# Attention scores before the spectral products: one wide pair and three single banks, two scan banks, and the division and the maxima's last steps at other places

## The chip, the cores and the metric

The kernel runs on one core of one Trainium2 chip. The metric is the device time of one execution in microseconds, given as the median of several executions. The traces are profiled executions of the same program.

## The reference

Two branches of a model are mixed by a gate, for 2048 rows of width 512 in float32:

```python
def reference(A_x, A_wqkv, A_wo, B_x, B_dft_seq_re, B_dft_seq_im, B_dft_hid_re, B_dft_hid_im, gate_w):
    x = A_x
    g = _sigmoid((x * gate_w).sum(-1, keepdims=True))
    # A: 32 heads of width 16
    q, k, v = ...                                  # x @ wqkv, cut into heads
    p = _softmax(einsum("bhqd,bhkd->bhqk", q, k) * 16 ** -0.5)
    a = einsum("bhqk,bhkd->bhqd", p, v) ... @ wo
    # B: Fourier mixing, the real part
    re = einsum("bsd,ed->bse", x, dft_hid_re)
    im = einsum("bsd,ed->bse", x, dft_hid_im)
    b = einsum("ts,bse->bte", dft_seq_re, re) - einsum("ts,bse->bte", dft_seq_im, im)
    return g * a + (1 - g) * b
```

## The kernel before, in words

The program has three parts. In the first, up to about 340 us, the projections to queries, keys and values and the first Fourier product are made, and beside them the first maxima of scores ("scans") for the softmax. Most products work on values split into a high and a low part of a narrower float format, so that one product becomes three matmuls of 64 rows each.

The second part is attention, 16 pairs of heads one after the other. A pair has 32 **steps**: two halves of the queries (1024 each) times 16 blocks of 128 keys. In a step the scores of the two heads (j = 0 and 1) against two chunks of 512 queries (c = 0 and 1) are made by four matmuls (L690), in the order that `ORDERS` gives: "e0" is the next score of head 0, "c0" the next scan of head 0, "s0" the next spectral matmul of row half 0. Head 0 uses rows 0 to 49 of the array, head 1 rows 64 to 113, so that two neighbours run beside each other. The scores go to PSUM, an exponential on ScalarE (`exponentials`, L672) takes them to SBUF, and `pv` (L702, "the value product") multiplies them with the values, summing over the keys in bank `pvb`. The value product of a step is issued after the scores of the second step behind it. Two steps are a **macro**, numbered m from 0 to 255.

A **scan** (L723) makes the scores of 128 queries against 512 keys, and VectorE reduces them to their maximum (L725). Scans run ahead of the pairs that use them. When a pair is scanned, `shift` gives five pieces of work: a reduction (L209), a transposition (L210), a cast (L211), a subtraction (L212) on VectorE, and a store of two DMAs on SyncE (L206). They are put on the list `late`, and the main loop takes them from it between the tokens of a macro. The query rows of a pair are loaded only when its scan is done, with a margin while `late` holds anything.

The first 42 macros (`SINGLES`) are 84 **single steps**: "e0 e1 c0 c1 e0 e1", then a value product, with no spectral matmuls. They use the pool `wide` of PSUM: two pairs of banks ("a" for chunk 0, "b" for chunk 1), each emptied by one exponential of 1024 columns, three single banks in turn for scans, and the bank `pvb`: eight in all. From macro 42 on `narrow()` replaces the pool: scores and scans share five banks that a planner of the program (`Banks`) hands out, each exponential takes 512 columns, and between the scores stand the spectral matmuls (L946) with two banks of their own, z0 and z1, in groups; `closing` holds groups that ended in a macro, and `group.close` has VectorE read their bank out (L855, L857, and L891 for the output product).

At the end of each half of a pair, `quotients` copies `pvb` to SBUF (`ob`, L735 on VectorE in the single steps, L737 on ScalarE later) and GpSimd gathers the sums by DMA (`lc<-ob`, L740). `divide` gives three pieces that the main loop runs at the head of a later macro, by the list `staged`: `invert` (a reciprocal on VectorE, L747, which waits for the gather, and a DMA, L748), `spread` (four DMAs on GpSimd, L752) and `scale` (three GpSimd operations, L755, L762 and L763, and two stores, L770, or for pair 14 the loads of its rows).

From macro 234 on the groups are the product with wo. `output_operands` loads its parts on SyncE; two of these tiles are first cleared (L791), then filled by four DMAs each (L793).

In the third part, after the last step, the last products are made and the rows are stored.

Of the kernel before, what the change touches and what calls it, by code (L numbers as in the profile page):

```python
# [10 lines left out]
F32 = mybir.dt.float32  # L11
# [7 lines left out]
P = 128  # L19
# [4 lines left out]
NP = H // 2  # L24
# [18 lines left out]
SINGLES = 42  # L43
# [17 lines left out]
def build(tc, x, xT, wqkv, wo, wrT, wiT, cr, ci, gate, out):  # L61
    nc = tc.nc
    with ExitStack() as ctx:
# [534 lines left out]
        with ExitStack() as pa:  # L598
# [6 lines left out]
            wide = pw.enter_context(tc.tile_pool(name="wide", bufs=1, space=PSUM, reuse_waits="tile"))  # L605
            pools = []

            def bank(tag, name="s"):
                return pools[0].tile([P, 512], F32, tag=tag, name=name)
# [11 lines left out]
            for s in range(NB - 4, NB):  # L621
                raw = ap.tile([P, D], F32, tag="take", name="abr", bufs=3)
# [36 lines left out]
            banks = Banks()  # L659
            es, waiting = {}, []  # L660
# [13 lines left out]
            pair = {}  # L674
# [3 lines left out]
            def score(j):  # L678

                step, c = divmod(scores[j], 2)  # L680
                scores[j] += 1
                p, h, kb, b = step // PERIODS, step % PERIODS // NB, step % NB, 64 * j
                rows, alone = used[p], step < 2 * SINGLES
                if alone:
                    if c not in pair:
                        pair[c] = wide.tile([P, 1024], F32, tag="ab"[c], name="s2")
                    ps = pair[c][:, j * 512:j * 512 + 512]
                else:
                    ps = bank(banks.take("e", j))
                nc.tensor.matmul(ps, rows.k[kb // 8][b:b + 50, kb % 8 * P:(kb % 8 + 1) * P],  # L690
                                 rows.q[h][b:b + 50, c * 512:c * 512 + 512], start=True, stop=True)
                es.setdefault(step, {})
                if alone and scores[1 - j] <= 2 * step + c:
                    return
                waiting.append((step, c, None, pair.pop(c)) if alone else (step, c, j, ps))
                exponentials()

            def pv(step):
                p, h, kb = step // PERIODS, step % PERIODS // NB, step % NB
                banks.step()  # L700
                for c, j, r in quads:
                    nc.tensor.matmul(pvb[r:r + VC, :], va[:, kb, 2 * p + j, :], es[step][c][0][:, j * 512:j * 512 + 512],  # L702
                                     start=kb == 0, stop=kb == NB - 1, tile_position=(0, r))
                unused.extend(i for e, i in es.pop(step).values())
                exponentials()
                if kb == NB - 1 and step < STEPS - 1:
                    m = step // 2 + 1
                    for n, f in zip((3, 6, 9) if m < SINGLES else (2, 4, 6) if p < NP - 1 else (2, 3, 4), divide(*quotients(p, h))):
                        staged.setdefault(m + n, []).append(f)

            scans, late, leaving = [FRONT, FRONT], [], []
# [1 line left out]
            def scan(j):  # L713

                n = scans[j]
                scans[j] += 1
                p, i = n // SCANS, n % SCANS
                qb, c, b = i // 4, i % 4, 64 * j
                rows = scanned[p]
                if p not in mx:  # L720
                    new_maxima(p)
                ps = wide.tile([P, 512], F32, tag=f"c{(2 * n + j) % 3}", name="s") if now[0] < SINGLES else bank(banks.take("c", j))
                nc.tensor.matmul(ps, rows.q[qb // 8][b:b + 48, qb % 8 * P:(qb % 8 + 1) * P],  # L723
                                 rows.k[c // 2][b:b + 48, c % 2 * 512:(c % 2 + 1) * 512], start=True, stop=True)
                nc.vector.tensor_reduce(mx[p][:, j, qb, c:c + 1], ps, axis=AX.X, op=ALU.max)  # L725
                if i == SCANS - 1 and min(scans) > n:
                    late.extend(shift(p))
                    leaving.extend(("scan", p, part) for part in ("k0", "k1", "q1"))
                elif i == SCANS // 2 - 1 and min(scans) > n:
                    leaving.append(("scan", p, "q0"))  # L730
# [49 lines left out]
            def output_operands():  # L780

                for n in range(2 * ND - 2):
                    b = [block(6 + 2 * n + i) for i in range(2)]
                    raw = (ap.tile([P, D], F32, tag="craw", name="wor", bufs=3) if n == ND - 2 else
                           ap.tile([P, D], F32, tag="take", name="wor", bufs=3))
                    if n < ND - 1:
                        nc.sync.dma_start(raw, wo[n * P:n * P + P, :].rearrange("(h e) m -> e h m", e=DH))
                    else:
                        base = D - (8, 4, 2)[n - ND + 1] * DH
                        if n >= ND:  # L790
                            nc.vector.memset(raw, 0.0)  # L791
                            for c, j, r in quads:
                                nc.sync.dma_start(raw[r:r + DH, :], wo[base + DH * j:base + DH * j + DH, :])  # L793
                        else:
                            for r in (0, 64):
                                nc.sync.dma_start(raw[r:r + 64, :],
                                                  wo[base:base + 64, :].rearrange("(h e) m -> e h m", e=DH))
                    raws_.append((raw, b))
                    if n % (ND - 1) == ND - 2:
                        yield  # L800
                        yield
                        for raw, b in raws_:
                            yield
                            nc.vector.tensor_copy(b[0], raw)
                            nc.vector.tensor_sub(b[1], raw, b[0].bitcast(F32))
                            (w2 if n < ND - 1 else w4).append(b)
                        raws_.clear()
                        yield
# [247 lines left out]
            for m in range(MACROS):  # L1056
                for step in (2 * m, 2 * m + 1):
                    part_b(step)
                now[0] = m
                for f in staged.pop(m, ()):  # L1060
                    f()
                if m == SINGLES - 1:
                    for _ in range(3):
                        load_unit(ap, "craw", 3)
                if m == SINGLES:
                    narrow()
                release(*leaving)
                leaving.clear()
                p, half = divmod(m, NB)
                if half == NB // 2:  # L1070
                    leaving.append(("use", p, "q0"))
                elif half == 0 and m:
                    leaving.extend(("use", p - 1, part) for part in ("k0", "k1", "q1"))
                prefetch(m)
                for ph, s in freed:
                    if ph == 0:
                        renew(s)
                    else:
                        if s == 2:
                            output_rows(0)  # L1080
                        if s == 11:
                            output_rows(1)
                        if s in (5, 7, 9, 10, 11, 12):
                            next(operands, None)
                freed.clear()
                if m >= OUTM:
                    next(operands, None)
                n = min(scans)
                want = planned(m)
                ready = min(TOTAL, scans_ready(m))  # L1090
                count_ = max(0, min(2 if m < SINGLES else 4, want - n, ready - n))
                if m < SINGLES:
                    for i in range(2):
                        for k, token in enumerate(ORDERS[(count_ + 1 - i) // 2].split()):
                            {"e": score, "c": scan}[token[0]](int(token[1]))
                            if late and k == 3:
                                late.pop(0)()
                        values(2 * m + i - 1)
                    continue
                for k, token in enumerate(ORDERS[count_, sizes[m]].split()):  # L1100
                    {"e": score, "c": scan, "s": fill}[token[0]](int(token[1]))
                    if late and k in (6, 13, 20):
                        late.pop(0)()
                for group, j, ps in closing:
                    group.close(j, ps)
                closing.clear()
                values(2 * m)
            assert min(scans) == TOTAL, scans
# [85 lines left out]
```

## Time and profile before

| | |
|---|---|
| median of three runs | 1720.14 us (1719.69 to 1720.67) |
| profiled execution | 1721.4 us, span 1719.6 us |
| mean granted clock of TensorE | 0.996 |
| busy: PE, PEld, DVE, ACT, POOL | 1700.7, 1006.6, 1240.3, 1351.3, 696.2 us |
| exponentials (L672) | 1880: 168 of 1024 columns, 1712 of 512 columns |
| scans in attention (L723, L725) | 1312 |
| first and last start of an exponential | 342.0 and 1700.3 us |

The span is the time from the first to the last instruction of the profiled execution. PE is TensorE's matmuls, PEld its weight loads, DVE VectorE, ACT ScalarE, POOL GpSimd and SP SyncE. A matmul that waits for its weights counts as busy. In a row of the timeline stand start and length in us, engine, line, operation, tiles (what is written, then what is read), the shape, the count of merged instructions, and in brackets the idle time of the engine before it with what ended it. In rows of waits stand the one that waited, whom it waited for, the sum in us, the times and the longest.

### The profile page before, as it was taken

To read this page: it belongs to the slowest core of one execution; us is meant where nothing else is said; L and a number is where in the kernel's file an instruction comes from. 1 tells how busy PE (TensorE), PEld (TensorE's weight loads), DVE (VectorE), ACT (ScalarE), POOL (GpSimd) and SP (SyncE) were. 2 spreads that over 40 slices of the span, in tenths; PEclk is the share of its full clock that TensorE was granted. 3 is DMA by queue.
4 is the path that set the end of the run, shared out by engine and by line. 5 is a ranking of instruction groups with operands and counts; after the bars stand their busy time and mean duration, and the time that the engine had idled before them with its cause. 6 is when DMAs were issued, how large, how long until landed. Compare 5 with 4: busy or idle time off the path is not lost.

```text
span 1719.6 us, 37003 instructions
## 1 busy us (share of the span) xinstructions
PE 1700.7 (99%) x13687; PEld 1006.6 (59%) x13687; DVE 1240.3 (72%) x2359; ACT 1351.3 (79%) x2447; POOL 696.2 (40%) x876
## 2 busy tenths in 40 slices
PE   9999999999999999999999999999999999999998
PEld 7777778733335555565555555555555555555554
DVE  5699899866677777777777777777777777776333
ACT  5689988799997777777777777777777777777785
POOL 1464201444564544444444444434444443443121
PEclk9999999999999999999999999999999999999999
DMA  7664234553352333232333256323332322335422
GB/s 277 224 231 156 70 121 142 176 177 124 116 155 83 95 99 96 64 110 69 88 88 95 75 164 206 107 82 106 97 95 87 119 78 86 113 93 162 128 55 100
DMA packets 140005, 206.61 MB, mean 120 GB/s; under 512 B 58848, under 2 KB 61392, under 8 KB 139824
## 3 DMA queue, kind: packets, MB, share of 16 engines
q1 hardware_dynamic: 97552, 173.76, 31.8%
q0 software_dynamic: 41696, 29.44, 6.4%
q8 instruction: 108, 1.77, 0.4%
q10 hardware_dynamic: 576, 1.05, 0.2%
q14 instruction: 73, 0.60, 0.1%
HBM read 137.89 MB, written 65.81 MB: 118 GB/s over the span
## 4 chain that ended last, share of the span: by engine, by line
PE 93%; DMA 1%; issue 1%; DVE 1%; ACT 1%; POOL 0%; SPq 0%; DVEq 0%; ACTq 0%; POOLq 0%
PE pvb L702 27%; PE z L946 21%; PE s L723 15%; PE s L690 14%; PE xy L342 5%; PE s L187 5%; PE xy L358 5%; DMA q_d<-el 0%; ACT e L672 0%; DVE y L891 0%; DMA wor<-wo 0%; DMA lc<-ob 0%; POOL xg L546 0%; DMA qs<-q_d 0%; PE s L219 0%
## 5 line engine op out<-in xcount | busy, mean ns | idle before, releaser
L672 ACT ACTIVATE e<-s 128x512 f32<-128x512 f32 (+1 forms) x1880 | 1064.4, 638 | 262.2 <-PE s L690 211.5
L725 DVE TENSOR_REDUCE mx<-s 128x1 f32<-128x512 f32 x1312 | 849.6, 687 | 328.8 <-PE s L690 220.5
L690 PE MATMUL s<-qs,ks 50*128 50x512 f32 x2048 | 645.3, 425 | 0.9 <-ACT e L672 0.7
L702 PE MATMUL pvb<-e,va 128*17 128x512 f32 x4096 | 497.9, 596 | 0.0
L723 PE MATMUL s<-ks,qs 48*128 48x512 f32 x1312 | 484.8, 418 | 1.2 <-DVE mx L725 0.7
L946 PE MATMUL z<-b,chi 64*128 64x512 f32 x2060 | 472.0, 392 | 0.0
L690 PEld LDWEIGHTS s<-qs,ks 50*128 50x128 f32 x2048 | 325.6, 185 | 159.3 <-ACT e L672 138.9
L723 PEld LDWEIGHTS s<-ks,qs 48*128 48x128 f32 x1312 | 213.5, 185 | 188.8 <-issue 119.1
L946 PE MATMUL z<-b,clo 64*128 64x512 f32 x1030 | 299.9, 392 | 0.0
L946 PEld LDWEIGHTS z<-b,chi 64*128 64x128 f32 x2060 | 281.9, 186 | 28.6 <-issue 1.1
L193 DVE CUSTOM_DVE_ANT_0 fold<-s,fold 128x512 f32<-128x512 f32 x368 | 242.6, 689 | 24.5 <-ACT fold L191 7.6
L187 PE MATMUL s<-ks,qs 48*128 48x512 f32 x736 | 236.4, 400 | 1.6 <-ACT fold L191 1.2
L245 POOL CAST chi<-craw 128x512 fp32r<-128x512 f32 x126 | 77.5, 615 | 379.9 <-PE z L946 359.6
L191 ACT ACTIVATE fold<-s 128x512 f32<-128x512 f32 x368 | 202.8, 605 | 29.4 <-PE s L187 28.2
L702 PEld LDWEIGHTS pvb<-e,va 128*17 128x17 f32 x4096 | 90.1, 96 | 210.4 <-issue 209.0
L246 POOL TENSOR_TENSOR clo<-craw,chi 128x512 fp32r<-128x512 f32 x126 | 162.1, 1286 | 10.7 <-PE s L723 0.3
L946 PEld LDWEIGHTS z<-b,clo 64*128 64x128 f32 x1030 | 157.6, 186 | 14.6
L740 POOL DMA_DIRECT2D lc<-ob x124 | 63.1, 514 | 249.8 <-ACT ob L737 208.5
L187 PEld LDWEIGHTS s<-ks,qs 48*128 48x128 f32 x736 | 134.9, 184 | 38.7 <-DVE mx L193 13.0
L358 PE MATMUL xy<-w,b 64*128 64x512 f32 x384 | 121.1, 399 | 0.0
L342 PE MATMUL xy<-w,b 64*128 64x512 f32 x384 | 116.9, 392 | 0.0
L891 DVE SCALAR_TENSOR_TENSOR y<-z,g,y 128x512 f32<-128x512 f32 x44 | 32.5, 750 | 70.1 <-PE z L946 68.4
(134 smaller groups left out, 1508.2 us busy)
## 6 DMA issues: line engine op xcount, KB each, us to landing
craw<-cr SPq DMA_DIRECT2D x64, 256.0 KB
craw<-ci SPq DMA_DIRECT2D x64, 256.0 KB
qs<-q_d SPq DMA_DIRECT2D x126, 128.0 KB
ks<-k_d SPq DMA_DIRECT2D x108, 128.0 KB
ab_d<-ab SPq DMA_DIRECT2D x32, 256.0 KB
y_d<-y SPq DMA_DIRECT2D x32, 256.0 KB
b<-bs_d SPq DMA_DIRECT2D x32, 256.0 KB
qs<-q_d SPq DMA_DIRECT2D x126, 64.0 KB
```

Of the source, the lines that this page charges most:

```text
L187: nc.tensor.matmul(ps, rows.q[qb // 8][b:b + 48, qb % 8 * P:(qb % 8 + 1) * P], rows.k[c // 2][b:b + 48, c % 2 * 512:(c % 2 + 1) * 512], st ...
L191: seen_by(nc.scalar.activation(fold[j], ps, AF.Relu))
L193: seen_by(nc.vector.tensor_tensor_reduce(out=fold[j], in0=ps, in1=fold[j], scale=1.0, scalar=-3.0e38, op0=ALU.add, op1=ALU.max, accum_out= ...
L246: sub(lo, raw, hi.bitcast(F32))
L342: ins = nc.tensor.matmul(ps, lhs[64:P], rhs[64:P], start=False, stop=last)
L358: nc.tensor.matmul(ps, lhs[0:64], rhs[0:64], start=n == 0, stop=False)
L672: nc.scalar.activation(e if j is None else e[:, j * 512:j * 512 + 512], ps, AF.Exp, scale=SCALE)
L690: nc.tensor.matmul(ps, rows.k[kb // 8][b:b + 50, kb % 8 * P:(kb % 8 + 1) * P], rows.q[h][b:b + 50, c * 512:c * 512 + 512], start=True, sto ...
L702: nc.tensor.matmul(pvb[r:r + VC, :], va[:, kb, 2 * p + j, :], es[step][c][0][:, j * 512:j * 512 + 512], start=kb == 0, stop=kb == NB - 1, ...
L723: nc.tensor.matmul(ps, rows.q[qb // 8][b:b + 48, qb % 8 * P:(qb % 8 + 1) * P], rows.k[c // 2][b:b + 48, c % 2 * 512:(c % 2 + 1) * 512], st ...
L725: nc.vector.tensor_reduce(mx[p][:, j, qb, c:c + 1], ps, axis=AX.X, op=ALU.max)
L946: nc.tensor.matmul(ps, pr_.lhs(j), pr_.rhs(j), start=group.count[j] == 1, stop=group.count[j] == group.size)
```

## The change

In the single steps chunk 0 keeps its pair of banks and its exponential of 1024 columns. Chunk 1 gets three single banks in turn for its two scores of a step, and two exponentials of 512 columns. Scans use two banks, one for each head. The banks are eight as before.

From macro 42 to the pair before the last the three pieces of the division run three, five and seven macros on, where they ran two, four and six on. The pieces of `shift` are no longer taken between the tokens of such a macro (after the 7th, 14th and 21st token) but at its end, behind the closing of groups: two of them, or one where a group closed. In the single steps they are taken as before. The two clearing operations move from VectorE to GpSimd.

```diff
@@ score
-                if alone:
+                if alone and c == 0:
                     if c not in pair:
-                        pair[c] = wide.tile([P, 1024], F32, tag="ab"[c], name="s2")
+                        pair[c] = wide.tile([P, 1024], F32, tag="a", name="s2")
                     ps = pair[c][:, j * 512:j * 512 + 512]
+                elif alone:
+                    ps = wide.tile([P, 512], F32, tag=f"s{(2 * step + j) % 3}", name="s")
                 else:
                     ps = bank(banks.take("e", j))
...
-                if alone and scores[1 - j] <= 2 * step + c:
+                if alone and c == 0 and scores[1 - j] <= 2 * step:
                     return
-                waiting.append((step, c, None, pair.pop(c)) if alone else (step, c, j, ps))
+                waiting.append((step, c, None, pair.pop(c)) if alone and c == 0 else (step, c, j, ps))
@@ pv
-                    for n, f in zip((3, 6, 9) if m < SINGLES else (2, 4, 6) if p < NP - 1 else (2, 3, 4), divide(*quotients(p, h))):
+                    for n, f in zip((3, 6, 9) if m < SINGLES else (3, 5, 7) if p < NP - 1 else (2, 3, 4), divide(*quotients(p, h))):
                         staged.setdefault(m + n, []).append(f)
@@ scan
-                ps = wide.tile([P, 512], F32, tag=f"c{(2 * n + j) % 3}", name="s") if now[0] < SINGLES else bank(banks.take("c", j))
+                ps = wide.tile([P, 512], F32, tag=f"c{j}", name="s") if now[0] < SINGLES else bank(banks.take("c", j))
@@ output_operands
-                            nc.vector.memset(raw, 0.0)
+                            nc.gpsimd.memset(raw, 0.0)
@@ the main loop
                 for k, token in enumerate(ORDERS[count_, sizes[m]].split()):
                     {"e": score, "c": scan, "s": fill}[token[0]](int(token[1]))
-                    if late and k in (6, 13, 20):
-                        late.pop(0)()
                 for group, j, ps in closing:
                     group.close(j, ps)
+                for _ in range(min(len(late), 1 if closing else 2)):
+                    late.pop(0)()
                 closing.clear()
                 values(2 * m)
```

## The prediction

> **What bounds the kernel now.** I read the page first, then busy time by stretch, then the waits and the timeline inside the stretch that the change touches most.
>
> ```profile
> span 1719.6 us, 37003 instructions
> ...
> PE 1700.7 (99%) x13687; PEld 1006.6 (59%) x13687; DVE 1240.3 (72%) x2359; ACT 1351.3 (79%) x2447; POOL 696.2 (40%) x876
> ```
>
> TensorE is called 99% busy, but a matmul that waits for its weights counts as busy too, so this row can't tell work from waiting. The weight loads' row (PEld) and the stretches can. After the stretch and its length, the next view gives busy time and instruction count of PE, PEld, DVE, ACT and POOL, the granted clock, DMA share and GB/s.
>
> ```profile
> 350.00:511.30 161.30, 160.76 (x1126) 49.42 (x1128) 108.02 (x178) 153.27 (x161) 81.58 (x118) 1.00 0.45 139
> 511.30:1591.20 1079.90, 1079.24 (x8860) 624.04 (x8858) 800.20 (x1275) 828.08 (x1568) 470.59 (x598) 1.00 0.35 103
> 1591.20:1599.80 8.60, 6.74 (x46) 4.08 (x45) 2.82 (x7) 4.78 (x11) 3.06 (x6) 0.80 0.36 102
> ```
>
> The first stretch holds 80 of the 84 single steps: 161.3/80 = 2.016 us a step, ScalarE busy for 95% of it, weight loads for 31%. The second is attention with spectral products between, where ScalarE has room (77%). The third is one macro (two steps) that lost time at a lowered clock. In the single steps the waits say who holds TensorE up (who waits, for whom, us in total, times, longest):
>
> ```profile
> PEld s L690 <- ACT e L672: 74.4, 127, 0.9
> ```
>
> That is the score's weight load waiting for an exponential to leave its two banks. Two steps in order of time (start, length, engine, line):
>
> ```profile
> 434.73 1.05 PE L702 MATMUL pvb<-e,va 128*17 128x512 f32 x8
> ...
> 435.71 0.51 PE L690 MATMUL s<-qs,ks 50*128 50x512 f32 x2
> ...
> 436.05 0.41 PE L723 MATMUL s<-ks,qs 48*128 48x512 f32 x2
> ...
> 436.28 0.40 PE L690 MATMUL s<-qs,ks 50*128 50x512 f32 x2
> 436.31 3.83 ACT L672 ACTIVATE e<-s 128x1024 f32<-128x1024 f32 x4 [0.19 <-PE s L690]
> 436.48 1.29 DVE L725 TENSOR_REDUCE mx<-s 128x1 f32<-128x512 f32 x2 [0.85 <-PE s L723]
> 436.62 1.05 PE L702 MATMUL pvb<-e,va 128*17 128x512 f32 x8
> ...
> 437.71 0.19 PEld L723 LDWEIGHTS s<-ks,qs 48*128 48x128 f32 x2
> 437.94 0.39 PE L723 MATMUL s<-ks,qs 48*128 48x512 f32 x2
> ...
> 438.20 1.94 ACT L672 ACTIVATE e<-s 128x1024 f32<-128x1024 f32 x2
> ...
> 438.30 0.19 PEld L690 LDWEIGHTS s<-qs,ks 50*128 50x128 f32 x2 [0.40 <-ACT e L672]
> ...
> 438.74 1.05 PE L702 MATMUL pvb<-e,va 128*17 128x512 f32 x8
> ...
> 439.72 0.50 PE L690 MATMUL s<-qs,ks 50*128 50x512 f32 x2
> ...
> 440.35 1.02 ACT L672 ACTIVATE e<-s 128x1024 f32<-128x1024 f32 x1 [0.21 <-PE s L690]
> ```
>
> From value product to value product: 436.62 - 434.73 = 1.89 us without a wait, then 438.74 - 436.62 = 2.12 with one; 4.01 for two, 2.00 a step. TensorE's own order costs 1.89. ScalarE makes four wide exponentials in 3.83 us: three starts apart plus one length, so (3.83 - 1.02)/3 = 0.94 apart, and 1.94 - 1.02 = 0.92 for the two from 438.20; 1.84 to 1.88 a step, and it idles about 0.2 in 4.0. So neither is the bound alone. The bound is a loop over two steps: the exponential of chunk 0 starts at 436.31, that of chunk 1 0.92 later and ends at 438.25; the next chunk-1 scores load at 438.30, the value product follows at 438.74, the next chunk-0 scores at 439.72, their exponential at 440.35. That is 4.04.
>
> **The single steps.** With three single banks in turn, the second chunk's first score needs the exponential of the step before last (far past), and its second score the first short exponential of the last step. That one starts 0.92 after 436.31 and lasts about 0.60:
>
> ```profile
> 547.63 1.58 ACT L672 ACTIVATE e<-s 128x512 f32<-128x512 f32 x3
> ...
> 546.49 4.40 ACT L672 ACTIVATE e<-s 128x512 f32<-128x512 f32 x8 [1.20 <-PE s L690]
> ```
>
> 436.31 + 0.92 + 0.60 + 0.05 = 437.88, while the score is due about 0.1 after the scan at 437.94. The loop opens. What is late next? Short exponentials stand (1.58 - 0.60)/2 = 0.49 apart in the first of these rows; (4.40 - 0.60)/7 = 0.54 in the second, which holds waits for scores. I take 0.49: ScalarE then needs 0.92 + 2 x 0.49 = 1.90 a step, against TensorE's 1.89. So 1.90, a gain of 0.10 in each of 80 steps: 8.0 us.
>
> The Trainium skill speaks against the split: "Perfetto Trace Analysis", section "Optimizing Scalar/DVE Operations", gives ScalarE a fixed cost of about 51 ns per PSUM operation and advises larger operations where the engine is saturated. By it one operation more a step would be about 4 us over the phase (an estimate); the rows give 2 x 0.49 - 0.92 = 0.06 a step. The same section says that splitting helps where an unsaturated engine causes bubbles elsewhere; the 0.2 idle in 4.0 puts this case there.
>
> The scans go from three banks to two. Chunk scans of a step are reduced one after the other: 1.29 from 436.48, so the second bank is free at 437.77; the next weight load came at 437.71 and could come at about 437.82. A score that waited for its weights (438.30) was followed by the value product 0.44 later, against 0.34 for one that didn't (436.28), so late weights cost 0.1, not a whole load: matmul at 437.93, seen at 437.94. Cost nought, but with no slack; behind a late scan stand, in TensorE's queue, the second scores and the value product. What lengthens VectorE's turn is then paid:
>
> ```profile
> L735 DVE COPY ob<-pvb 128x512 f32<-128x512 f32 x5 | 3.5, 692 | 1.1 <-PE pvb L702 1.0
> ```
>
> Of a step of 1.90 the reductions leave 0.61, so each of five copies comes 0.1 late: 0.5 us. Single steps: 8.0 - 0.5 = 7.5.
>
> **The spectral part.** Its macros run at one pace unless VectorE, in order, is held:
>
> ```profile
> 1048.20 1.91 PE L702 MATMUL pvb<-e,va 128*17 128x512 f32 x16
> ...
> 1054.41 1.05 PE L702 MATMUL pvb<-e,va 128*17 128x512 f32 x8
> ...
> 1099.25 1.91 PE L702 MATMUL pvb<-e,va 128*17 128x512 f32 x16
> ...
> 1104.82 1.91 PE L702 MATMUL pvb<-e,va 128*17 128x512 f32 x16
> ...
> 1111.28 1.05 PE L702 MATMUL pvb<-e,va 128*17 128x512 f32 x8
> ...
> 1051.17 0.25 DVE L747 RECIPROCAL lc<-lc 128x16 f32<-128x16 f32 x1 [0.70 <-DMA lc<-ob]
> ...
> 1109.22 0.98 DVE L211 CAST chi<-mt 128x32 fp32r<-128x32 f32 x1
> ```
>
> A normal macro is 1104.82 - 1099.25 = 5.57. The one to 1054.41 took 6.21: the reciprocal at its head waited 0.70 for its DMA with scans queued behind it. Staged three macros on instead of two it has 5.6 us more, and the wait goes: 0.6. The macro to 1111.28 took 6.46: shift steps stood between scans, one of them 0.98 long. At the macro's end they lie under the two value products (1.91), for which no scan bank is asked: 0.9. If that cover fails they cost what they do now. The shift ends up to two macros later, and with it the query rows' loads that wait for an empty list; the scans run macros ahead of use, so I cost that at nothing.
>
> ```profile
> 1586.16 1.91 PE L702 MATMUL pvb<-e,va 128*17 128x512 f32 x16
> ...
> 1591.23 1.91 PE L702 MATMUL pvb<-e,va 128*17 128x512 f32 x16
> ...
> 1595.00 0.49 PE L946 MATMUL z<-b,b 64*128 64x512 f32 x1 [1.86 <-DVE y L891]
> ...
> 1599.79 1.91 PE L702 MATMUL pvb<-e,va 128*17 128x512 f32 x16
> ...
> 1592.06 0.25 DVE L747 RECIPROCAL lc<-lc 128x16 f32<-128x16 f32 x1 [4.66 <-DMA lc<-ob]
> 1592.37 1.03 DVE L791 MEMSET wor<- 128x512 f32 x2
> ...
> 1593.35 1.59 DVE L891 SCALAR_TENSOR_TENSOR y<-z,g,y 128x512 f32<-128x512 f32 x2
> ...
> 1597.00:1599.00 2.00, 2.00 (x12) 1.64 (x10) 0.00 (x0) 1.32 (x3) 0.00 (x0) 0.50 0.31 70
> ```
>
> Here the reciprocal waited 4.66 us for a gather that competed with large loads; two memsets followed; then the closing of a product group (L891), for which TensorE's next group sat idle 1.86 us, after which the clock was 0.50. This macro took 8.56, the one before 5.07: 3.5 lost. Staged a macro later the reciprocal stands behind the closing, and the memsets leave VectorE, so this goes whole. The Trainium skill, "TensorE: Matmul & The Clock Gate", Part 1, ties the lowered clock to an idle window of about 3.4 us; the rows show it after 1.86, so I let the clock's part go with the wait. By the Trainium skill's window only the idle 1.86 would be won, 1709.3 in all, inside the forecast's own range.
>
> The rest of the staging: one DMA of the inverse, four of the spread, three GpSimd operations and two stores (or four loads on SyncE for pair 14) come one macro later, still ahead of the next half's at eight macros; pair 14's rows are wanted at macro 250 and loaded at 247 instead of 246. The memsets now wait for their tile on GpSimd, before its inverse's DMA, and SyncE's weight loads wait for them; a GpSimd memset isn't in the trace, and between VectorE's 0.5 and double that it moves loads used macros later: nothing.
>
> Sum: 7.5 + 0.6 + 0.9 + 3.5 = 12.5. The profiled execution took 1721.4 us (span 1719.6); by the sum it would take 1708.9. The median shown is 1720.1, so 1707.6.
>
> **Rivals.** *The spectral delays return elsewhere* (GpSimd's memsets or late shift steps hold another closing): only the single steps gain, 1720.1 - 7.5 = 1712.6. For it: VectorE is in order and its waits move easily. *The single steps stay at 2.00*: short exponentials at 0.54 (0.92 + 1.08 = 2.00), or the scan's ring of two banks costing the 0.1 without slack. Then only 5.0: 1715.1. *ScalarE was saturated already*, and the step grows by the split's price, 0.06: 80 x 0.06 = 4.8 against 5.0, no change, 1719.9. The Trainium skill's section on scalar and DVE operations, cited above, is this rule. Against it stands the 0.2 idle. *Slower*: a short exponential behind a wide one isn't overlapped and takes its whole 0.60; the step is 0.92 + 1.20 = 2.12, so 80 x 0.12 = 9.6 lost against 5.0 won: 1724.7. It decides from a step of 2.00 + 5.0/80 = 2.06, shorts 0.57 apart. Against it: wide ones do overlap (0.92 apart at a length of 1.02), and so do shorts (0.49 at 0.60).
>
> **How the numbers follow.** Forecast 0.60 (1704 to 1711: TensorE's 1.89 and no lost copy give 1.3 more, smaller shift delays 1 or 2), spectral delays back 0.14, single steps unchanged 0.15, saturated 0.03, slower 0.08. The range 1704.0 to 1715.5 takes in the first three but for their edges. A measurement here tells about 0.2% (3.4 us) from no change: faster 0.89, same 0.03, slower 0.08.
>
> **What would show it.** Right: value products 1.90 apart in the single steps with no alternation, short exponentials about 0.49 apart, the score's wait for ScalarE down from 74.4 to under 20; no macro of 6.2, 6.5 or 8.6 and no clock of 0.50 near the end. Wrong: scan weights waiting for VectorE in each step, ScalarE without gaps at over 2.0 a step, or a new wait of TensorE for VectorE at a macro's end.

## The result, and the profile after

The changed kernel takes 1706.39 us (median of four runs, 1704.14 to 1708.41) against 1719.91; the ratio is 0.9921, 95% interval 0.9904 to 0.9938. Run again beside its parts it took 1707.51 against 1720.05, ratio 0.9923 (0.9906 to 0.9941). The forecast was 1707.6, faster.

The profiled execution took 1705.85 us, span 1704.1. Its stretches between the same value products as in the three rows of before (the second one, the 82nd, and the two that bound the macro of the lowered clock), in the same columns; line numbers of the main loop are two higher in the changed kernel (L692 is L690 of before):

```profile
349.01:500.92 151.91, 151.91 (x1122) 56.94 (x1121) 107.77 (x178) 151.79 (x241) 81.85 (x119) 1.00 0.49 146
500.92:1579.16 1078.24, 1078.24 (x8861) 623.54 (x8859) 802.99 (x1276) 828.27 (x1569) 470.89 (x599) 1.00 0.36 103
1579.16:1584.23 5.07, 5.07 (x45) 2.83 (x43) 1.79 (x5) 4.13 (x10) 1.09 (x2) 1.00 0.49 121
```

The 80 single steps went from 161.3 to 151.9 us: 1.90 a step. ScalarE, which had been idle for 5% of them, is now busy for all of them. The second stretch is 1.7 shorter, the third went from 8.6 to 5.1 with the clock at 1.00; 1.0 us lies before the first row. Two single steps in order of time:

```profile
429.31 5.98 ACT L672 ACTIVATE e<-s 128x512 f32<-128x512 f32 x9
...
430.24 0.40 PE L692 MATMUL s<-qs,ks 50*128 50x512 f32 x2
...
430.57 1.05 PE L704 MATMUL pvb<-e,va 128*17 128x512 f32 x8
...
431.55 0.19 PEld L692 LDWEIGHTS s<-qs,ks 50*128 50x128 f32 x2 [0.85 <-ACT e L672]
431.56 0.50 PE L692 MATMUL s<-qs,ks 50*128 50x512 f32 x2
431.66 0.30 PEld L725 LDWEIGHTS s<-ks,qs 48*128 48x128 f32 x2
431.89 0.40 PE L725 MATMUL s<-ks,qs 48*128 48x512 f32 x2
431.90 0.32 PEld L692 LDWEIGHTS s<-qs,ks 50*128 50x128 f32 x2
432.13 0.40 PE L692 MATMUL s<-qs,ks 50*128 50x512 f32 x2
...
432.33 1.29 DVE L727 TENSOR_REDUCE mx<-s 128x1 f32<-128x512 f32 x2 [0.60 <-PE s L725]
...
432.46 1.05 PE L704 MATMUL pvb<-e,va 128*17 128x512 f32 x8
```

Value products start 432.46 - 430.57 = 1.89 apart, and no second score waits: its weights load at 431.90, as soon as the scan streams (431.89), where they came 0.36 after it before (438.30 after 437.94). The exponentials from 355 to 500 us, grouped by shape (count, busy us, mean ns, idle before):

```profile
L672 ACT ACTIVATE e<-s 128x512 f32<-128x512 f32 x153 | 90.9, 704 | 0.0
L672 ACT ACTIVATE e<-s 128x1024 f32<-128x1024 f32 x77 | 86.7, 1126 | 0.1
```

No idle time in front of either, and both last longer than before (704 for 598 ns, 1126 for 1023): ScalarE always has the next one at hand.

The two macros with a delay in the spectral part, and VectorE in them:

```profile
1037.62 1.91 PE L704 MATMUL pvb<-e,va 128*17 128x512 f32 x16
...
1043.24 1.05 PE L704 MATMUL pvb<-e,va 128*17 128x512 f32 x8
...
1093.64 1.91 PE L704 MATMUL pvb<-e,va 128*17 128x512 f32 x16
...
1099.25 1.05 PE L704 MATMUL pvb<-e,va 128*17 128x512 f32 x8
...
1040.00 4.07 DVE L727 TENSOR_REDUCE mx<-s 128x1 f32<-128x512 f32 x6
1043.98 0.24 DVE L749 RECIPROCAL lc<-lc 128x16 f32<-128x16 f32 x1
...
1094.69 0.21 DVE L210 STREAM_TRANSPOSE mt<-m 128x32 f32<-128x32 f32 x1
1096.02 4.07 DVE L727 TENSOR_REDUCE mx<-s 128x1 f32<-128x512 f32 x6 [1.11 <-PE s L692]
```

Both take 5.62 and 5.61, where they took 6.21 and 6.46. The six reductions run in one piece; the reciprocal comes a macro later and waits for nothing, the shift's transposition stands ahead of the scans, in VectorE's free time. At the end:

```profile
1579.06 1.61 DVE L893 SCALAR_TENSOR_TENSOR y<-z,g,y 128x512 f32<-128x512 f32 x2 [3.65 <-PE z L948]
1580.59 0.18 DVE L212 TENSOR_TENSOR clo<-mt,chi 128x32 fp32r<-128x32 f32 x1
1580.69 0.25 DVE L749 RECIPROCAL lc<-lc 128x16 f32<-128x16 f32 x1
...
POOL wor L793 <- DMA y_d<-y: 4.6, 1, 4.6
```

The closing of the product group is first, and the reciprocal follows it. The wait for the tile now stands on GpSimd (last row, from the waits: 4.6 us), where it holds up nothing that shows: the macro takes its usual 5.07.

### The profile page after: what moved, and what is told of

Its sections match the earlier page's. It is cut to its first block, busy times and chain, and to the rows that moved or that the text cites. A ratio compares the mean times of both kernels' runs of the same rounds, so it can differ in the third digit from the quotient of the medians.

```text
span 1704.1 us, 37092 instructions
## 1 busy us (share of the span) xinstructions
PE 1687.6 (99%) x13687; PEld 1016.8 (60%) x13687; DVE 1241.5 (73%) x2357; ACT 1349.6 (79%) x2531; POOL 697.2 (41%) x878
## 3 DMA queue, kind: packets, MB, share of 16 engines
q10 hardware_dynamic: 576, 1.05, 0.2%
## 4 chain that ended last, share of the span: by engine, by line
PE 95%; ACT 1%; DVE 1%; issue 0%; DMA 0%; POOL 0%; DVEq 0%; ACTq 0%
PE pvb L704 28%; PE z L948 22%; PE s L725 16%; PE s L692 13%; PE xy L342 6%; PE s L187 5%; PE xy L358 5%; DMA q_d<-el 0%; DVE y L893 0%; DVE fold L193 0%; PE s L219 0%; ACT fold L191 0%; ACT e L672 0%; ACT c L374 0%; ACT xg L547 0%
## 5 line engine op out<-in xcount | busy, mean ns | idle before, releaser
L692 PE MATMUL s<-qs,ks 50*128 50x512 f32 x2048 | 639.9, 418 | 1.0 <-ACT e L672 1.0
L692 PEld LDWEIGHTS s<-qs,ks 50*128 50x128 f32 x2048 | 330.2, 184 | 135.1 <-ACT e L672 116.0
L725 PEld LDWEIGHTS s<-ks,qs 48*128 48x128 f32 x1312 | 221.9, 185 | 187.8 <-issue 101.2
L948 PEld LDWEIGHTS z<-b,clo 64*128 64x128 f32 x1030 | 157.5, 186 | 14.5
L187 PEld LDWEIGHTS s<-ks,qs 48*128 48x128 f32 x736 | 134.6, 184 | 36.5 <-DVE mx L193 12.1
```

What stands on the lines that cost most here:

```text
L948: nc.tensor.matmul(ps, pr_.lhs(j), pr_.rhs(j), start=group.count[j] == 1, stop=group.count[j] == group.size)
```

## The experiments

Executions differ by up to 6 us in when attention starts (the table's first column), so medians don't tell apart edits of 1 us. Part of that is TensorE's clock: the four that start after 352 us are the four whose granted clock was 0.50 for 3.4 us at about 58 us. The places tell them apart: the table gives, for one profiled execution of each kernel, the start of the second value product, the 80 steps up to the 82nd, the macros of 6.21, 6.46 and 8.56 us, all from the starts of the value products, and the ratio of times with its interval.

| kernel | start | 80 steps | 6.21 | 6.46 | 8.56 | ratio |
|---|---|---|---|---|---|---|
| before | 350.0 | 161.3 | 6.21 | 6.46 | 8.56 | 1 |
| after | 349.0 | 151.9 | 5.61 | 5.61 | 5.07 | 0.9921 (0.9904 to 0.9938) |
| after, again | 347.9 | 152.1 | 5.60 | 5.61 | 5.07 | 0.9923 (0.9906 to 0.9941) |
| single steps only | 349.3 | 152.0 | 6.39 | 6.45 | 5.36 | 0.9934 (0.9914 to 0.9955) |
| all but the single steps | 352.8 | 162.2 | 5.59 | 5.61 | 5.07 | 0.9983 (0.9972 to 0.9994) |
| division only | 349.6 | 161.1 | 5.61 | 6.44 | 5.62 | 0.9991 (0.9982 to 1.0001) |
| shift only | 352.1 | 161.2 | 5.92 | 5.58 | 6.24 | 0.9993 (0.9983 to 1.0002) |
| clearing only | 352.7 | 162.1 | 5.95 | 6.45 | 5.07 | 0.9996 (0.9985 to 1.0006) |
| two scan banks only | 349.4 | 161.2 | 5.63 | 6.45 | 6.34 | 0.9997 (0.9988 to 1.0007) |
| two single banks | 348.9 | 163.4 | 5.59 | 5.61 | 5.07 | 0.9997 (0.9988 to 1.0007) |
| five single banks | 349.7 | 157.5 | 5.61 | 5.61 | 5.07 | 0.9960 (0.9946 to 0.9974) |
| after, small copy | 349.4 | 160.5 | 5.59 | 5.59 | 5.07 | 0.9988 (0.9978 to 0.9999) |
| before, small copy | 353.9 | 161.5 | 5.97 | 6.43 | 5.71 | 1.0005 (0.9996 to 1.0015) |
| two scan banks, small copy | 349.7 | 166.8 | 6.37 | 6.45 | 6.14 | one run |

The same holds for the 80 steps. In four kernels (all but the single steps, clearing only, five single banks, two scan banks with the copy) the clock was still lowered for most of the first of them. That step took 2.91 to 3.12 us there and 1.89 to 2.23 in the others, so about 1 us of these four sums isn't the edit's. For five single banks the granted clock in it is 0.60:

```profile
349.66:352.62 2.96, 2.96 (x16) 0.85 (x15) 1.09 (x3) 1.68 (x4) 2.80 (x4) 0.60 0.55 176
```

**The changed kernel again.**

> The changed kernel once more, beside its parts. Both theories: about 13.5 us under the kernel before (1704 to 1708). The theory of three separate causes (a loop of two steps opened in the single steps, a wait taken from the macro at the end, two short delays in the spectral part) expects the same places in the trace as in its first profile.

As expected, at the same places.

**Single steps only.** The edits in `score` and `scan`, nothing else.

> Only the new banks of the single steps (scores and scans); division, shift and clearing as before. Theory, the opened loop: steps 1.89 us apart, 80 x 0.11 = 9 us less; the macro near the end still 8.6 us, with the lowered clock, and the ones of 6.2 and 6.5 us still there, so about 1720 - 9 = 1711. Rival, the parts depend on each other (the earlier start moves the transfers, so that the long macro at the end vanishes by itself): about 1706.

1708.55 us, lower than expected. The steps gain 9.3 us, as in the full change; the two middle macros keep their delays. But the end macro took 5.36 with nothing done to it; the reciprocal and the two clearing operations stand in front of the closing as before:

```profile
1580.78 0.25 DVE L749 RECIPROCAL lc<-lc 128x16 f32<-128x16 f32 x1 [3.00 <-DMA lc<-ob]
1583.72 0.50 PE L948 MATMUL z<-b,b 64*128 64x512 f32 x1 [0.21 <-DVE y L893]
```

The wait for the gather is 3.00 here, not 4.66, and TensorE idles 0.21, not 1.86. The rival, that the earlier start moved the transfers, isn't excluded for this 5.36. But the kernels below that keep both waits and get no earlier start took 5.71 to 6.34, and no other profile shows the 8.56.

**All but the single steps.** The edits in `pv`, `output_operands` and the main loop.

> Only the three edits of the spectral part (division three, five and seven macros on, shift at the macro's end, clearing on GpSimd); single steps as before. Theory: single steps 2.00 to 2.02 us apart, no macro over 5.7 us, 5.0 us less: 1715. Rival, the delays only moved: 1718 to 1720.

1716.59 us. The steps stay at 162.2 (about 161.2 without the low clock in the first), all three macros are normal. The rival falls: the delays went, and nothing took their place.

**Division only.**

```diff
-(2, 4, 6) if p < NP - 1
+(3, 5, 7) if p < NP - 1
```

> Only the division three, five and seven macros on. Theory: the reciprocal's wait held the closing, so the macro of 8.56 us falls to about 5.1 and that of 6.21 to 5.6: 4.1 less, 1715.9; the macro of 6.5 stays. Rival, the two clearing operations on VectorE hold the closing by themselves, since they wait for their tile until 1592.4: the macro stays over 6 us and only 1 to 2.5 us are won.

1719.27 us: a miss for the theory. The macro of 6.21 is normal, but at the end:

```profile
1590.15 1.91 PE L702 MATMUL pvb<-e,va 128*17 128x512 f32 x16
1592.53 0.50 PE L946 MATMUL z<-b,b 64*128 64x512 f32 x1 [0.47 <-DVE y L891]
...
1590.44 0.48 DVE L791 MEMSET wor<- 128x512 f32 x1 [3.58 <-DMA y_d<-y]
1590.84 0.13 DVE L212 TENSOR_TENSOR clo<-mt,chi 128x32 fp32r<-128x32 f32 x1
1590.88 1.59 DVE L891 SCALAR_TENSOR_TENSOR y<-z,g,y 128x512 f32<-128x512 f32 x2
```

The reciprocal is gone from in front, and the second clearing waits in its place, 3.58 us for its tile; TensorE is still held 0.47. The rival was right about this wait, though it put the macro at over 6 us (it took 5.62).

**Shift only.**

> Only the shift's pieces at the macro's end. Theory: the macro of 6.46 us falls to 5.6 and the small delays at other shifts mostly go: 0.9 to 1.3 us less, 1718.8; the long macro at the end stays. Rival, the pieces now hold the closing of groups or the next scans: no gain, with macros over 5.7 us behind the shifts.

1718.57 us; the macro of 6.46 falls to 5.58 and the end macro stays long (6.24), as the theory says.

**Clearing only.** `nc.vector.memset(raw, 0.0)` becomes `nc.gpsimd.memset(raw, 0.0)`.

> Only the two clearing operations on GpSimd. Theory: the reciprocal still waits until 1592, the closing comes 1.0 us earlier, so the macro falls from 8.56 to about 7.5: 1.0 less, 2.5 if the clock's dip goes too. Rival, the clearing operations were the cause: the macro falls to about 5.1, 3.5 less.

1719.22 us; the end macro is 5.07: the rival's number, and a miss for the theory's 7.5. But the reciprocal still stood in front. It waited 3.65 and ended just as the closing was due:

```profile
1594.33 1.91 PE L702 MATMUL pvb<-e,va 128*17 128x512 f32 x16
...
1594.16 0.25 DVE L747 RECIPROCAL lc<-lc 128x16 f32<-128x16 f32 x1 [3.65 <-DMA lc<-ob]
1594.33 0.13 DVE L212 TENSOR_TENSOR clo<-mt,chi 128x32 fp32r<-128x32 f32 x1
1594.38 1.59 DVE L891 SCALAR_TENSOR_TENSOR y<-z,g,y 128x512 f32<-128x512 f32 x2
```

In the first profile of before the gather landed 1.0 later against the value product; by this order it would still have held the closing, which no run here shows. So two waits stood in a row, and each edit takes one away. That the closing needs both edits is argued from this order, not shown. All six executions with both edits show 5.07.

**Two scan banks only.** `tag=f"c{(2 * n + j) % 3}"` becomes `tag=f"c{j}"`, scores as before.

> Only the scans on two banks instead of three; both chunks still on bank pairs (one bank is unused). Theory: the loop over the two exponentials sets 2.00 us a step and the ring of two banks has just no slack: no change, 1720. Rival, the smaller ring costs by itself: 2.05 to 2.1 a step, 4 to 8 us more.

161.2 for the 80 steps: no change, as the theory says.

**Two single banks.** In the changed kernel `tag=f"s{j}"` for the second chunk, and the scans back on three.

> The changed kernel with two single banks for the second chunk (one for each head) instead of three, and three for the scans. Theory, the loop: the second head's score now waits for the second short exponential of the step before, which starts 0.92 + 0.49 after the wide one and ends 0.60 later, so the loop closes again: 2.04 us a step, 80 x 0.15 = 12 us over the changed kernel, 1718. Rival, the split into shorter exponentials is what helps: 1.90 a step, 1706.

163.4/80 = 2.04 us a step and 1718.50 us, the theory's numbers: the loop is closed again, and short exponentials alone help nothing. The second head's weights wait by themselves, and the starts alternate (2.16, 1.90):

```profile
430.71 1.05 PE L704 MATMUL pvb<-e,va 128*17 128x512 f32 x8
...
432.45 0.18 PEld L692 LDWEIGHTS s<-qs,ks 50*128 50x128 f32 x1 [0.23 <-ACT e L672]
...
432.87 1.05 PE L704 MATMUL pvb<-e,va 128*17 128x512 f32 x8
...
434.77 0.62 PE L704 MATMUL pvb<-e,va 128*17 128x512 f32 x4
```

**Five single banks.** `tag=f"s{(4 * step + 2 * c + j) % 5}"` for all scores, no wide exponential.

> The changed kernel with five single banks in turn for all four scores of a step, and four exponentials of 512 columns. Theory, ScalarE and TensorE now stand level and each short exponential costs 0.48 to 0.49: 4 x 0.48 to 0.49 = 1.92 to 1.96 us a step, 2 to 6 us over the changed kernel. Rival, TensorE's order alone is the bound: 1.89 a step, no change.

157.5/80 = 1.97 a step, or 1.96 without the 1 us of low clock in the first; 0.49 for each exponential, and 1713.04 us, against 1706.39 and 1707.51 for the mixed kernel. ScalarE without idle time:

```profile
L672 ACT ACTIVATE e<-s 128x512 f32<-128x512 f32 x298 | 146.2, 940 | 0.0
```

So the one wide exponential is worth its two banks: 4.6 us over the single steps, with that 1 us taken off.

**A small copy between the reductions**, in the changed kernel, in the kernel before, and in the kernel before with two scan banks:

```diff
+                if j and now[0] < SINGLES:
+                    nc.vector.tensor_copy(idle, ones)
                 nc.vector.tensor_reduce(mx[p][:, j, qb, c:c + 1], ps, axis=AX.X, op=ALU.max)
```

> The changed kernel with one more small copy on VectorE (128x32) in each single step, between the two reductions, into a tile that nothing reads. Theory, the ring of two scan banks has no slack: the second bank comes free 0.1 to 0.2 later and the step grows by as much, to 1.97 us: 5 to 8 us over the changed kernel. Rival, VectorE's 0.6 us of free time a step hides it: no change.

> The kernel before with the same small copy in each single step. Theory: with three scan banks a scan has a step's time of slack, and the step stays at 2.00 to 2.02 us: no change, 1720. Rival, VectorE's turn is on the path before as well: 5 to 8 us more.

> The kernel before with scans on two banks and the small copy between the two reductions: the ring of two without the opened loop. With the copy alone, or with two banks alone, the 80 steps took 161.5 and 161.3 us. Theory, the ring is what has no slack: the copies that last 0.5 to 1.2 us now hold scan weights back, and the 80 steps take 3 to 5 us more, 164.5 to 166.5. Rival, it was the level stand of ScalarE and TensorE in the changed kernel that let the copies through: still about 161.5.

The 80 steps took 160.5 (8.6 more), 161.5 (no change) and 166.8 (5.6 more than two banks alone, of which 1 us is the low clock in the first step, so 4.6, within the 3 to 5 expected; one profile). So it is the ring of two that has no slack, with the loop open or closed. Of waits for VectorE's reductions the weight loads of scans show, in the first and third:

```profile
PEld s L726 <- DVE mx L730: 6.1, 14, 1.0
```

```profile
PEld s L724 <- DVE mx L728: 5.9, 10, 0.9
```

In the kernel before with the copy there is no such row.

## Why the prediction was right, point by point

**The loop: right.** A loop of two steps through the second chunk's exponential set 2.00 us, and the third single bank opens it. With two single banks it closes again at the 2.04 that the same rows give. The split as such brings nothing.

**The step: right (1.90), the gain under-sized.** 9.3 us came where the sum had 8.0 - 0.5. The sum took 2.00 for the steps before, from one pair of them; the stretch's 2.016 stood in the row above it and holds, among others, three pauses of about 0.25 (starts of value products 2.34 to 2.38 apart instead of 2.12) that the opened loop hides: after, none of the 80 are over 2.06 apart. The whole difference is 1.3 us. Steps without a copy of `pvb` took 1.89, TensorE's own pace, instead of ScalarE's 1.90: another 0.8. The five copies cost 0.10 to 0.17 each, near the 0.1 that was put down.

**ScalarE and TensorE level: right, and the Trainium skill's caution with it.** "Perfetto Trace Analysis", section "Optimizing Scalar/DVE Operations", warns of a fixed cost for each operation where ScalarE is saturated. It wasn't saturated before and is now, and the kernel of five single banks shows the rule: one more split costs 0.06 a step (1.96 against 1.90).

**Two scan banks without slack: right.** Two banks alone cost nothing; with a small copy they do.

**Division and shift in the middle: right.** The shift's 0.9 is the same in all executions without the edit (6.43 to 6.46) and goes with it alone. The division's 0.6 was again one draw: without the edit that macro took 5.63 to 6.39, with it 5.59 to 5.61.

**The end macro: right in its place, over-sized in its price.** Of the term of 3.5 us, 0 to 1.3 is usual: seven other executions with one or both of the old waits in front of the closing took 5.07, 5.36, 5.62, 5.71, 6.14, 6.24 and 6.34 against 5.07. The reciprocal's wait varies with the gather (3.00 to 4.66 us where it stood in front), and only at its longest did the clock fall. The step that failed was to take one execution's wait for a DMA as the kernel's. It also named the reciprocal as the wait and the clearing as a mere follower; but the clearing waits for a tile of its own, as the 3.58 us of the division alone shows.

The sum came close because the two errors cancel: 1.8 too little in the single steps, 2 to 3.5 too much at the end. That is luck. The two profiles also differ in that attention began about 1 us earlier in the one of after, which is within what executions differ by.

**One sign was wrong.** The score's wait for ScalarE was to fall under 20 us. It stands at 64.7 in 145 us of single steps (74.4 in 140 us that were nearly all single steps before):

```profile
PEld s L692 <- ACT e L672: 64.7, 76, 0.9
```

All 76 of these waits are 0.85 to 0.92 long. They are the time that weight loads are idle during each value product, and the view puts it down to the last semaphore awaited. The row at 431.55 above is one of them: its matmul starts at 431.56, before the value product's end (430.57 + 1.05 = 431.62), so nothing was held up. The prediction had read the row of before wrongly too: 65 of its 127 waits, 55.3 of the 74.4 us, were of this kind and not scores waiting for their banks. Stalls can be only among the short ones, like the 0.40 at 438.30, and none of these is left. The matmul starts should have been named as the sign.

## What to carry to other kernels

Where two engines both show room and the step is still longer than either needs, follow one buffer around: the loop through its release sets the pace, and one more buffer in turn can be worth more than a shorter operation, as it was here. Trade banks from rings that need them for the bandwidth to ones that need them for the loop, and count what slack the giver keeps. A wait for a DMA seen once is one draw: before it is priced, look at it in several executions, and look for the next wait behind it on the same engine.

## What the runs showed of the hardware

The small copy of 128x32 takes 0.17 us as a rule, but up to 1.23 when it begins while GpSimd is at an operation on a whole tile; it ends with it (412.73 + 1.15 = 413.88, against 412.54 + 1.29 = 413.83). A cast of GpSimd does this as well as an operation on two tensors. In each of the three profiles with the copy 21 copies began so, with more than 0.13 us of GpSimd's operation left, and all ended 0.03 to 0.05 us after it. From the timelines of the changed kernel with the copy, VectorE and GpSimd:

```profile
412.73 1.15 DVE L729 COPY idle<-ones 128x32 f32<-128x32 f32 x1
```

```profile
412.54 1.29 POOL L760 TENSOR_TENSOR ob<-ob,rb 128x512 f32<-128x512 f32 x1
```

The shift's cast of 0.98 in the macro of 6.46 us was the same: it ended at 1110.20, GpSimd's operation at 1110.16. The Trainium skill, "Perfetto Trace Analysis", section "Optimizing Scalar/DVE Operations", says that the two engines share a read port, which a two-port operation of VectorE holds alone. These rows agree that the two engines get in each other's way, but here it is VectorE that waits. In the changed kernel with the copy each of the eleven steps over 2.2 us holds a copy of 0.47 us or more, and these steps make up 5.9 of the 8.6 us lost.

TensorE's clock fell to 0.50 after one idle time of 1.86 us, and stayed at 1.00 after one of 1.19 (two scan banks only):

```profile
1593.16 0.50 PE L946 MATMUL z<-b,b 64*128 64x512 f32 x1 [1.19 <-DVE y L891]
...
1594.00:1596.00 2.00, 2.00 (x20) 1.73 (x18) 0.00 (x0) 1.93 (x5) 1.05 (x3) 1.00 0.55 128
```

The length of one idle time doesn't decide it alone. At about 57 us the clock stayed at 1.00 after an idle time of 2.51 (two scan banks with the copy, the rows below) and fell after one of 1.79 (clearing only). At the start of attention, between 343 and 349 us, it fell in 13 of the 14 profiles with no idle time over 1 us near it.

```profile
56.49 0.50 PE L358 MATMUL xy<-b,w 64*128 64x512 f32 x1 [2.51 <-DVE el L450]
...
58.00:62.00 4.00, 4.00 (x38) 3.60 (x36) 1.41 (x3) 1.14 (x2) 0.00 (x0) 1.00 0.56 201
```

The idle window of about 3.4 us in the Trainium skill, "TensorE: Matmul & The Clock Gate", Part 1, wasn't needed for it here, as one unbroken idle time: the longest before a fall within the kernel was 2.83 us. What share of a window must be idle these runs don't tell.
